# Dealing Fourier butterflies anew over projection units, and a third piece by VectorE in three units more

## The chip, the core and the metric

The kernel runs on one core of a Trainium2 chip. A core has TensorE (PE; its weight loads are listed as PEld), VectorE (DVE), ScalarE (ACT), GpSimd (POOL) and SyncE (SP, which only issues transfers here), each with a queue of its own that it works off in order, and 16 DMA engines. Engines wait for each other by semaphores. The metric is the device time of one execution in microseconds (us); lower is better.

## The reference

Two independent computations, side by side in the output. A is a memory-augmented attention over 2048 rows of 576 with 32 heads of 18, in 4 segments of 512; B is a filter in the two-dimensional Fourier space.

```python
def _A_ref(x, wq, wk, wv, wo, beta):
    q, k, v = ...            # x @ wq, x @ wk, x @ wv, split into heads and 4 segments
    phi = lambda t: jnp.where(t > 0, t + 1.0, jnp.exp(t))
    for s in range(N):
        qs, ks, vs = q[:, :, s], k[:, :, s], v[:, :, s]
        logits = jnp.einsum("bhqd,bhkd->bhqk", qs, ks) * scale + mask
        p = _softmax(logits, axis=-1)
        a_dot = jnp.einsum("bhqk,bhkd->bhqd", p, vs)
        num = jnp.einsum("bhld,bhde->bhle", phi(qs), M)
        den = jnp.einsum("bhld,bhd->bhl", phi(qs), z)[..., None] + 1e-6
        outs.append(g * num / den + (1.0 - g) * a_dot)
        M = M + jnp.einsum("bhld,bhle->bhde", phi(ks), vs)
        z = z + jnp.einsum("bhld->bhd", phi(ks))
    return o @ wo

def _B_ref(x, w_r, w_i):
    X = jnp.fft.rfft2(x, axes=(-2, -1)) * (w_r + 1j * w_i)
    return jnp.fft.irfft2(X, s=(S, D), axes=(-2, -1))
```

## The kernel before

The kernel has four stages, one after the other on TensorE: the forward transform of B, the projections of A (q, k and v), the inverse transform of B, and the attention of A. The order of instructions on each engine is written out by hand; what is issued first on an engine runs first there.

The 2048-point transform of B is cut into parts that are matmuls (forward and inverse stage) and parts of radix 4 that VectorE does on the array Z in on-chip memory: butterflies (L210), twiddle factors (L227 on VectorE, fed by L221 and L222 on ScalarE), the product with the filter (L247, L249, L253, L255). These parts are written as Python generators that yield after each VectorE instruction, 200 steps in all, which the class `Pace` deals out in small numbers between the work of A. Each step is one VectorE instruction on 128 x 580 numbers, but for one step in each set of twiddles that starts with ScalarE alone. 14 steps are dealt in the forward stage. `projections` (L540) deals all that are left but 8, and the inverse takes the rest.

`projections` runs four groups g of 512 rows. In each it runs 13 units i: nine of q and k (i = 0 to 8, `qk_unit`, L466), each 128 of the 1152 columns of q and k, then four of v (i = 9 to 12, `v_unit`, L503), each 128 rows. A matmul in full single precision is made of 14 passes over high and low parts (`passes`, L454).

A q or k unit's result lies in a bank of PSUM, the accumulation memory. There are five such banks for these units (tag `pj`); they are used in turn, and a v unit takes two of them, one for each half of its columns. The result is written as three bfloat16 pieces into `sp3`. ScalarE copies the first piece out (L476). VectorE subtracts it from the bank in place (L483). ScalarE copies the second piece (L487). The third piece is made in one of two ways: either TensorE subtracts the second piece in the bank, by a matmul with a negative unit matrix `nid` (L491), and ScalarE copies the rest out (L492); or VectorE subtracts and writes in one instruction (L489). Before the change VectorE does it in the odd units of groups 1 to 3. In most units ScalarE and VectorE also compute phi (L479, L480, L482), and the phi of k is transposed on TensorE (L500). On v units TensorE also adds up M and z (L523), VectorE masks them (L531) and GpSimd adds them on (L535 to L539).

The loop of `projections` in unit i issues: the first half of unit i on TensorE; one advance of every unit that is open; 70% of the steps of the unit's share w; one more advance; the second half of unit i; the other 30% of w. By the two advances, unit i-1 gets its L476 and phi in the first and L482 and L483 in the second, and unit i-2 gets L487 in the first and its third piece in the second. On VectorE the order in unit i is thus: the 70%, L489 of unit i-2 if it has one, L482 and L483 of unit i-1, the 30%. The share is in proportion to a weight, 1 for a unit of q or k and 2.1 for one of v (L560).

In the last group a hook issues the splitting of Z for the inverse (`ysplit`, L278): ScalarE copies the high part Y (L284), and VectorE subtracts for the low part (L285) in the units i = 10, 11 and 12. Before it splits, it takes steps until the butterflies that it needs are issued. The inverse starts with matmuls on Y (L300), of which ScalarE copies the high part (L330) and VectorE subtracts the low part (L332), and goes on with L311.

Of the kernel before, what the change touches and what calls it, by code (L numbers as in the profile page):

```python
# [389 lines left out]
class ATT:  # L390
# [63 lines left out]
    def passes(s,out,g,wt,cs,xs,swap):  # L454

        wh,wl=s.wh[wt],s.wl[wt]; xh=[s.xh[g,t] for t in range(5)]; xl=[s.xl[g,t] for t in range(4)]
        L=[]
        for t in range(4):
            L+=[(wh[:,t,cs],xh[t][:,xs]),(wh[:,t,cs],xl[t][:,xs]),(wl[:,t,cs],xh[t][:,xs])]
        L+=[(wh[:,4,cs],xh[4][:,xs]),(wl[:,4,cs],xh[4][:,xs])]  # L460
        if swap:
            L=[(b,a) for a,b in L]
        for i,(a,b) in enumerate(L):
            s.nc.tensor.matmul(out,a,b,start=i==0,stop=i==len(L)-1)  # L464
            if i==6 and not swap: yield
    def qk_unit(s,g,mt,tp,pp):  # L466

        nc=s.nc
        ps=pp.tile([128,512],F32,name="pj",tag="pj")
        yield from s.passes(ps,g,"wqk",slice(128*mt,128*mt+128),slice(0,512),False)  # L470
        yield
        sp3=tp.tile([128,3,512],BF,name="sp3",bufs=3)
        r0=0 if (g>0 or mt>4) else 64
        r1=128 if (g<3 or mt<4) else 64
        if (g==0 and mt<4) or (g==3 and mt>4): r1=r0
        nc.scalar.copy(sp3[:,0],ps)  # L476
        if r1>r0:
            e=tp.tile([128,512],F32,name="ex")
            nc.scalar.activation(e[r0:r1],ps[r0:r1],AF.Relu,scale=-1.0)  # L479
            nc.scalar.activation(e[r0:r1],e[r0:r1],AF.Exp,scale=-1.0)  # L480
        yield
        if r1>r0: nc.vector.scalar_tensor_tensor(e[r0:r1],ps[r0:r1],0.0,e[r0:r1],op0=OP.max,op1=OP.add)  # L482
        nc.vector.tensor_tensor(ps,ps,sp3[:,0],op=OP.subtract)  # L483
        qr=min(r1,128 if mt<4 else (64 if mt==4 else 0))
        if qr>r0: nc.sync.dma_start(s.pqD[g][128*mt:128*mt+qr],e[:qr])
        yield
        nc.scalar.copy(sp3[:,1],ps)  # L487
        yield
        if g>0 and mt%2: nc.vector.tensor_tensor(sp3[:,2],ps,sp3[:,1],op=OP.subtract)  # L489
        else:  # L490
            nc.tensor.matmul(ps,s.nid,sp3[:,1],start=False,stop=True,skip_group_check=True)  # L491
            nc.scalar.copy(sp3[:,2],ps)  # L492
        nc.sync.dma_start(s.qkD[g][128*mt:128*mt+128],sp3)
        if r1<=r0: return
        k0=max(r0,0 if mt>4 else (64 if mt==4 else 128))
        if k0>=r1: return
        n=r1-k0; c0=128*mt+k0-576
        pt=pp.tile([128,4,128],F32,name="ptr",tag="pt")
        for tb in range(4):
            nc.tensor.transpose(pt[:,tb,:n],e[k0:r1,128*tb:128*tb+128],s.ident[k0:r1,k0:r1])  # L500
        yield
        nc.scalar.copy(s.pk[:,:,c0:c0+n],pt[:,:,:n])
# [37 lines left out]
    def projections(s,xp,tp,pp,wv,pace,hook):  # L540

        live=[]
        s.nid=wv.tile([128,128],BF,name="nid"); s.nc.scalar.activation(s.nid,s.ident,AF.Copy,scale=-1.0)
        lw=s.load_w("wv",576,wv,xp,288,"xl",4)
        def advance():
            for l in list(live):
                try: next(l)
                except StopIteration: live.remove(l)
        tot=pace.left-8
        for g in range(4):  # L550
            if g<3: xq=[s.xprep(g+1,t,(xp,s.x0)[g%2],xp,[128,512],"xst",2) for t in range(5)]
            for i in range(13):
                u=s.qk_unit(g,i,tp,pp) if i<9 else s.v_unit(g,i-9,tp,pp)
                if i==4 and g<3: s.pk=tp.tile([128,4,576],F32,name="pk",bufs=1)
                next(u)
                hook(g,i)
                next(lw,None); next(lw,None)
                if g<3 and i in (4,6,8,10,12): next(xq[(i-4)//2])
                if g<3 and i in (1,3,5,7,9): next(xq[(i-1)//2])
                w=tot/(36+16*2.1)*(1.0 if i<9 else 2.1)  # L560
                advance()
                pace.take(w*.7)
                advance()
                next(u)
                pace.take(w*.3)
                live.append(u)
        while live: advance()
# [573 lines left out]
```

## Time and profile before

| | |
|---|---|
| runs shown | 718.73, 719.6, 716.9 us; median 718.73 |
| profiled execution | 715.83 us, its span 714.1 us |
| PE busy | 678.0 us, 95% of the span |
| DVE busy | 552.8 us, 77% |
| ACT busy | 444.4 us, 62% |
| POOL busy | 209.1 us, 29% |
| granted TensorE clock | 1.00 over the span |

The span is the time from the first to the last instruction that the profiler records. Matmuls overlap: one lasts longer than the time until the next starts, so a busy TensorE is read by how many matmuls start in a stretch, and a wait of TensorE by the time from one start to the next. Times in a row of a time line are counted from the start of the span.

### The profile page before, as it was taken

Reading aid. Unit: us, or ns where it says so; the run is one execution under the profiler, and the core shown is the slowest. Engines: PE = TensorE matmul, PEld = TensorE weight load, DVE = VectorE, ACT = ScalarE, POOL = GpSimd, SP = SyncE. Lnnn points to the kernel's source line nnn. Section 1 sums busy time; section 2 is a strip of 40 time slices with the busy share of each in tenths; the row PEclk is TensorE's granted clock in tenths of the full one; section 3 lists DMA queues with packets and bytes.
Section 4 is the critical chain, followed back from the end, with each engine's and each line's share of the span. In section 5 each row is a group of like instructions: output and inputs, shape, how many; then the busy total and the mean of one; then the engine's idle time right before and its main releaser. Section 6 shows DMA issues by size and latency. Waiting matters only on the chain.

```text
span 714.1 us, 14181 instructions
## 1 busy us (share of the span) xinstructions
PE 678.0 (95%) x4867; PEld 498.0 (70%) x4867; DVE 552.8 (77%) x1227; ACT 444.4 (62%) x1000; POOL 209.1 (29%) x409
## 2 busy tenths in 40 slices
PE   5999999999999999999999999999999999998997
PEld 4999769879879779999844444444566445664677
DVE  6999989799799699787587878887566876668153
ACT  3657685575575564444487777777556676568631
POOL 2110000100100211465165434554242762237200
PEclk9999999999999999999999999999999999999999
DMA  9876536545473568899547666676547765341331
GB/s 344 277 224 200 157 125 192 182 162 181 136 238 127 164 209 278 204 232 226 167 112 180 173 163 148 176 177 172 134 121 181 172 164 132 104 138 43 99 100 66
DMA packets 83245, 121.04 MB, mean 170 GB/s; under 512 B 11353, under 2 KB 50631, under 8 KB 83037
## 3 DMA queue, kind: packets, MB, share of 16 engines
q1 hardware_dynamic: 76580, 104.11, 51.4%
q0 software_dynamic: 6592, 16.03, 8.1%
q8 instruction: 38, 0.62, 0.4%
q14 instruction: 35, 0.28, 0.1%
HBM read 81.78 MB, written 38.24 MB: 168 GB/s over the span
## 4 chain that ended last, share of the span: by engine, by line
PE 66%; DVE 14%; ACT 6%; DMA 6%; issue 4%; POOL 2%; SPq 0%; DVEq 0%; ACTq 0%; POOLq 0%
PE pv L716 9%; PE pj L464 7%; PE po L858 7%; PE pjv L464 7%; PE s L643 5%; PE i L300 4%; PE i L311 4%; PE s L651 4%; PE s L686 3%; DVE junk L647 2%; PE s L690 2%; PE po L888 2%; DMA x<-qkD 2%; DVE pj L483 2%; PE c L163 2%
## 5 line engine op out<-in xcount | busy, mean ns | idle before, releaser
L647 DVE CUSTOM_DVE_ANT_0 junk<-s,mask 128x512 bf16<-128x512 f32 (+1 forms) x256 | 141.5, 553 | 58.1 <-PE s L643 46.6
L653 DVE TENSOR_REDUCE mx<-s 128x4 f32<-128x512 f32 x128 | 87.9, 686 | 16.3 <-PE s L652 14.8
L687 ACT ACTIVATE P<-s 128x512 f32<-128x512 f32 x128 | 77.2, 603 | 23.3 <-PE s L686 20.4
L716 PE MATMUL pv<-P,vs 128*32 128x512 f32 (+3 forms) x1024 | 82.0, 438 | 0.0
L692 ACT ACTIVATE P<-s 128x512 f32<-128x512 f32 x128 | 77.0, 602 | 6.7 <-PE s L691 3.6
L696 ACT ACTIVATE P<-s 128x256 f32<-128x256 f32 x128 | 49.6, 387 | 50.1 <-PE s L695 50.1
L699 POOL TENSOR_SCALAR_AFFINE_SELECT P<-P 128x512 f32<-128x512 f32 x116 | 69.3, 633 | 6.2 <-ACT P L687 6.0
L716 PEld LDWEIGHTS pv<-P,vs 128*32 128x32 f32 x1024 | 26.8, 109 | 44.7 <-issue 42.0
L464 PE MATMUL pj<-x,wqkh 128*128 128x512 f32 x162 | 55.9, 406 | 0.0
L513 POOL MEMSET vt<- 128x32 f32 x16 | 2.4, 161 | 150.9 <-PE pm L523 123.7
L210 DVE TENSOR_TENSOR t<-Z 128x580 f32<-128x580 f32 x64 | 46.1, 755 | 0.1
L210 DVE TENSOR_TENSOR Z<-t 128x580 f32<-128x580 f32 x64 | 45.8, 755 | 0.1
L643 PE MATMUL s<-Ks,Qs 108*128 108x512 bf16 (+1 forms) x128 | 42.2, 329 | 0.0
L487 ACT CAST sp<-pj 128x512 bf16<-128x512 f32 x36 | 21.0, 585 | 30.0 <-DVE pj L483 30.0
L142 PE MATMUL f<-ftab,eh 128*128 128x290 f32 (+1 forms) x160 | 31.2, 313 | 8.9 <-DMA ftab<-ftab 8.9
L300 PE MATMUL i<-civ,Y 128*128 128x256 f32 (+1 forms) x288 | 37.9, 284 | 1.3 <-DVE T L332 1.3
L300 PEld LDWEIGHTS i<-civ,Y 128*128 128x128 f32 (+1 forms) x288 | 35.8, 181 | 1.6 <-DVE T L332 1.6
L311 PE MATMUL i<-itab,T 128*128 128x290 f32 (+1 forms) x224 | 36.4, 311 | 0.0
L668 POOL CAST mh<-mg 128x16 bf16<-128x16 f32 x32 | 6.8, 214 | 100.0 <-ACT mg L666 69.3
L464 PEld LDWEIGHTS pj<-x,wqkh 128*128 128x128 f32 x162 | 30.4, 188 | 7.7 <-issue 1.0
L464 PE MATMUL pj<-x,wqkl 128*128 128x512 f32 x90 | 35.6, 395 | 0.0
L464 PE MATMUL pj<-xh,wqkh 128*128 128x512 f32 x90 | 35.6, 395 | 0.0
(214 smaller groups left out, 1854.5 us busy)
## 6 DMA issues: line engine op xcount, KB each, us to landing
qkD<-sp SPq DMA_DIRECT2D x36, 384.0 KB
Ks<-qkD SPq DMA_DIRECT2D x72, 144.0 KB
x<-qkD SPq DMA_DIRECT2D x60, 144.0 KB
Qs<-qkD SPq DMA_DIRECT2D x60, 144.0 KB
xin<-xb SPq DMA_DIRECT2D x16, 384.0 KB
cfw<-cfw POOLq DMA_DIRECT2D x16, 384.0 KB, 4.3
civ<-civ POOLq DMA_DIRECT2D x16, 384.0 KB, 7.6
vs<-vD SPq DMA_DIRECT2D x16, 330.0 KB
```

Source lines behind the costliest of these rows:

```text
L210: v.tensor_tensor(o,a,b,op=op)
L300: nc.tensor.matmul(p[:m,k],Y[i][:,q,c*128:c*128+m],cc[:,hl,o:o+256],start=n==0,stop=n==5)
L311: nc.tensor.matmul(p,x,t,start=n==0,stop=n==6)
L464: s.nc.tensor.matmul(out,a,b,start=i==0,stop=i==len(L)-1)
L643: nc.tensor.matmul(out,Q[:108,h,128*i:128*i+128],K[:108,h,:128*(i+1)],start=True,stop=True)
L647: nc.vector.tensor_tensor_reduce(out=junk[:,:w],in0=src,in1=s.mask[:,512-w:],scale=1.0,scalar=-3.0e38, op0=OP.add,op1=OP.max,accum_out=s.m ...
L653: nc.vector.tensor_reduce(out=s.mx[k][:,hh],in_=pa.rearrange("p (b c) -> p b c",c=128),axis=mybir.AxisListType.X,op=OP.max)
L687: nc.scalar.activation(P[0][:,hh],p0,AF.Exp,scale=SC)
L692: nc.scalar.activation(P[1][:,hh],p1,AF.Exp,scale=SC)
L699: if k<29: nc.gpsimd.affine_select(out=x,in_=x,pattern=pat+[[1,128]],compare_op=OP.is_ge,fill=0.0,base=0,channel_multiplier=-1)
L716: nc.tensor.matmul(s.pvt[32*hh:32*hh+32,128*j:],vt[:,j,19*h:19*h+32],mv[0][:,hh,mv[1]],start=j==0,stop=j==2,skip_group_check=True)
L858: nc.tensor.matmul(ps,a[t][:r,c],b[:r,t,w],start=i==0,stop=i==14)
```

## The change

A unit's third piece is made by VectorE in unit 8 of groups 1 to 3 too, beside the odd units. The share of steps is worked out with other weights: 2.6 for a unit of v instead of 2.1, and 0.75 instead of 1 for a unit of q or k whose third piece is VectorE's. The sum of the weights in the divisor follows (15 units have 0.75).

```diff
+    def third(s,g,mt): return g>0 and (mt%2 or mt==8)
     def qk_unit(s,g,mt,tp,pp):
...
         nc.scalar.copy(sp3[:,1],ps)
         yield
-        if g>0 and mt%2: nc.vector.tensor_tensor(sp3[:,2],ps,sp3[:,1],op=OP.subtract)
+        if s.third(g,mt): nc.vector.tensor_tensor(sp3[:,2],ps,sp3[:,1],op=OP.subtract)
         else:
             nc.tensor.matmul(ps,s.nid,sp3[:,1],start=False,stop=True,skip_group_check=True)
             nc.scalar.copy(sp3[:,2],ps)
...
-                w=tot/(36+16*2.1)*(1.0 if i<9 else 2.1)
+                w=tot/(36-15*.25+16*2.6)*(2.6 if i>8 else .75 if s.third(g,i) else 1.0)
                 advance()
                 pace.take(w*.7)
                 advance()
```

## The prediction

> **What bounds the kernel now.** I read the page's head first, then a table of stages, the waits of TensorE, the time line of VectorE at the end of the stage, and the groups for prices. The change touches one stage, the projections, which run from 70.8 us to about 284 us. In the table the columns after the stretch are its length and the busy time of PE, PEld, DVE, ACT and POOL with their instruction counts, then granted clock, DMA share and GB/s.
>
> ```profile
> span 714.1 us, 14181 instructions
> ```
> ```profile
> 70.80:106.20 35.40, 32.98 (x148) 25.14 (x147) 32.49 (x55) 28.10 (x63) 0.35 (x4) 1.00 0.43 135
> ...
> 124.50:159.10 34.60, 33.94 (x164) 26.87 (x163) 29.47 (x50) 22.35 (x42) 3.25 (x14) 1.00 0.50 168
> 159.10:177.80 18.70, 18.63 (x144) 18.37 (x143) 18.53 (x28) 9.86 (x23) 0.34 (x4) 1.00 0.60 193
> ...
> 230.50:264.00 33.50, 32.67 (x151) 25.96 (x150) 26.70 (x45) 18.86 (x37) 3.75 (x10) 1.00 0.56 178
> 264.00:284.00 20.00, 19.41 (x150) 19.08 (x148) 19.84 (x32) 9.86 (x23) 5.27 (x16) 1.00 0.88 287
> ```
>
> The stretches are: q and k units of group 0, q and k of group 1, v of group 1, q and k of group 3, v of group 3. TensorE is busy nearly throughout, so it sets the pace; it loses 2.42, 0.66, 0.07, 0.83 and 0.59 us in them. VectorE has slack in q and k of groups 1 and 3 (5.1 and 6.8 us), but none in the last v stretch (0.16 us idle in 20). That last row speaks against putting more there.
>
> Where TensorE loses time in q and k shows in its time line, with the idle time before an instruction and its releaser in brackets:
>
> ```profile
> 80.09 0.38 PE L491 MATMUL pj<-sp,nid 128*128 128x512 bf16 x1 [0.93 <-ACT sp L487]
> ...
> 95.00 0.38 PE L491 MATMUL pj<-sp,nid 128*128 128x512 bf16 x1 [0.78 <-ACT sp L487]
> ...
> 99.94 0.38 PE L491 MATMUL pj<-sp,nid 128*128 128x512 bf16 x1 [0.71 <-ACT sp L487]
> ...
> 149.23 0.38 PE L491 MATMUL pj<-sp,nid 128*128 128x512 bf16 x1 [0.66 <-ACT sp L487]
> ...
> 202.08 0.38 PE L491 MATMUL pj<-sp,nid 128*128 128x512 bf16 x1 [0.38 <-ACT sp L487]
> ...
> 247.76 0.38 PE L491 MATMUL pj<-sp,nid 128*128 128x512 bf16 x1 [0.20 <-ACT sp L487]
> ...
> 255.30 0.38 PE L491 MATMUL pj<-sp,nid 128*128 128x512 bf16 x1 [0.63 <-ACT sp L487]
> ```
>
> All seven are the matmul of L491, late because ScalarE's L487 waited for VectorE's L483, queued behind butterflies. A matmul lasts 0.39 us but the next starts 0.23 us after it, so each bracket hides 0.16 us more; the seven cost 4.29 + 7 x 0.16 = 5.4 us.
>
> VectorE in turn runs dry where a v stretch ends:
>
> ```profile
> 130.87 0.69 DVE L482 SCALAR_TENSOR_TENSOR ex<-pj,ex 128x512 f32<-128x512 f32 x1 [3.46 <-ACT ex L480]
> ...
> 184.00 0.69 DVE L482 SCALAR_TENSOR_TENSOR ex<-pj,ex 128x512 f32<-128x512 f32 x1 [2.25 <-ACT ex L480]
> ...
> 236.63 0.69 DVE L482 SCALAR_TENSOR_TENSOR ex<-pj,ex 128x512 f32<-128x512 f32 x1 [3.71 <-ACT ex L480]
> ```
>
> These 2 to 4 us at the start of groups 1, 2 and 3 are what the first three v stretches can take more of for nothing.
>
> **The change part by part.** Prices: groups, shapes kept apart, then three rows of the chain of waits.
>
> ```profile
> L210 DVE TENSOR_TENSOR Z<-t 128x580 f32<-128x580 f32 x56 | 39.8, 755 | 0.1
> L483 DVE TENSOR_TENSOR pj<-pj,sp 128x512 f32<-128x512 f32 x36 | 24.8, 688 | 0.1
> ...
> L492 ACT CAST sp<-pj 128x512 bf16<-128x512 f32 x24 | 13.9, 578 | 4.0 <-PE pj L491 3.6
> ...
> L489 DVE TENSOR_TENSOR sp<-pj,sp 128x512 bf16<-128x512 f32 x12 | 8.2, 681 | 0.0
> ```
> ```profile
> 80.46 3.27 PE pj L464 x14
> 83.73 0.23 PE pj L491
> ...
> 108.84 3.71 PE pjv L464 x28
> ```
>
> A q or k unit costs TensorE 3.27 us, a v unit 3.71, the L491 matmul 0.23. Four butterflies in a row end after 2.77 us (row below), so one costs VectorE (2.77 - 0.755) / 3 = 0.67; L489 and L483 start 0.60 apart, so 0.60 each.
>
> *The new deal.* By the code there are 200 steps, 14 are dealt before the stage, 8 kept for after it: 178 to deal. Before, a unit of q or k gets 178/69.6 = 2.56 and one of v 5.37. After, 178/73.85 = 2.41, 1.81 where VectorE makes the third piece, and 6.27 in v. I counted which step falls where. Between the first and the fifth unit's L483 of groups 1, 2 and 3 there are now 8, 8 and 9 steps instead of 11, 10 and 11. The single late L491 of group 1 (0.66 + 0.16 = 0.82), that of group 2 (0.54) and the second of group 3 (0.79) need less than 0.67 x 2 of relief, so I take them as gone: 2.15 us gained. The first of group 3 has as many steps ahead as before (5) and stays. In group 0 the count of steps up to unit 8's L483 is the same (26), and the first late L491 has the same steps before it. The second loses two ScalarE operations of a twiddle that move a unit on; I take its 0.78 as gained and leave the others, between 0 and 2.9 us (all three brackets with their 0.16).
>
> *More in v, groups 0 to 2.* Four steps more per stretch, 2.7 us, hidden in the 2.25 to 3.71 us of VectorE's idle above. Were that cover gone, each step would cost 0.67. What is late next is the L482 of the following group's first unit and, behind it, that unit's L483, L487 and L491.
>
> *Third piece in unit 8 of groups 1 to 3.* It removes 0.23 us of TensorE and 0.58 of ScalarE, adds 0.60 of VectorE. In group 1 the matmul also opened a hole: 165.16 to 165.74 for a 0.13 us matmul, so 0.45 gained there, 0.23 in group 2. But unit 8's bank of the five is now freed by VectorE's L489, which stands behind the first butterflies of the v stretch, and the fifth allocation after it, the first half of the third v unit, takes that bank. For group 1:
>
> ```profile
> 159.30 0.29 PE L464 MATMUL pjv<-wvh,xh 128*128 128x288 f32 x1
> ...
> 165.16 0.29 PE L464 MATMUL pjv<-wvl,xh 128*128 128x288 f32 x1
> ...
> 165.74 0.60 PE L500 MATMUL ptr<-ident,ex 128*128 128x128 f32 x4
> ...
> 168.04 0.29 PE L464 MATMUL pjv<-wvh,xh 128*128 128x288 f32 x1
> ```
> ```profile
> 164.16 0.69 DVE L483 TENSOR_TENSOR pj<-pj,sp 128x512 f32<-128x512 f32 x1
> ```
>
> Unit 8 ends at 159.30, the third v unit starts at 168.04, or 8.3 us later without the matmul and its hole. VectorE ended L483 of unit 8 at 164.76. With four steps fewer since the group began (2.7 us) and the group starting 0.8 earlier, that is 161.3. Behind it stand 7 steps (4.7), L437 (0.6) and L489 (0.6): the bank is free at 167.2. TensorE, 0.8 + 0.8 earlier, wants it at 157.7 + 8.3 = 166.0. A new wait of 1.2 us: the whole TensorE queue stands behind it, and VectorE is not held. Bounds: 0, up to 3.1 (rivals). In group 2 only 5 steps stand between; I take nothing.
>
> So up to the end of group 3's unit 8, TensorE is ahead by 0.78 + 0.82 + 0.45 - 1.2 + 0.54 + 0.23 + 0.79 = 2.4 us.
>
> *The last v stretch.* No idle time to fill here: VectorE also splits Y.
>
> ```profile
> 261.88 0.69 DVE L483 TENSOR_TENSOR pj<-pj,sp 128x512 f32<-128x512 f32 x1
> 262.48 2.10 DVE L210 TENSOR_TENSOR t<-Z 128x580 f32<-128x580 f32 x3
> ...
> 265.85 0.68 DVE L489 TENSOR_TENSOR sp<-pj,sp 128x512 bf16<-128x512 f32 x1
> 266.45 0.69 DVE L483 TENSOR_TENSOR pj<-pj,sp 128x512 f32<-128x512 f32 x1
> ...
> 278.46 1.09 DVE L285 TENSOR_TENSOR Y<-Z,Y 128x512 fp32r<-128x512 f32 x2
> 279.47 2.77 DVE L210 TENSOR_TENSOR Z<-t 128x580 f32<-128x580 f32 x4
> ...
> 282.83 0.68 DVE L332 TENSOR_TENSOR T<-i,T 128x512 fp32r<-128x512 f32 x1
> ...
> 284.00 0.69 DVE L332 TENSOR_TENSOR T<-i,T 128x512 fp32r<-128x512 f32 x1
> ```
> ```profile
> 263.92 0.30 PE L464 MATMUL pjv<-wvh,xh 128*128 128x288 f32 x1
> ...
> 278.99 4.42 PE L300 MATMUL i<-civ,Y 128*128 128x256 f32 x36
> 284.75 2.41 PE L300 MATMUL i<-civ,Y 128*128 128x256 f32 x18 [1.34 <-DVE T L332]
> ```
>
> From 262.48 VectorE works without a pause to the second L332, and TensorE resumes at 284.75 when that is done: VectorE sets the end of the stage. From unit 7's L483 to the first L332 stood 24 steps; now 29 do, and a second L489: 5 x 0.67 + 0.60 = 4.0 us more. The L483 of unit 7 can itself be about 0.4 us earlier against TensorE, since the butterflies before it are fewer. So TensorE resumes 4.0 - 0.4 - 2.4 = 1.2 us later than before. The bank wait comes here too. On the clock of before, VectorE is through unit 7's L483 at 262.1, through 5 steps, L489 and unit 8's L483 at 266.7, and through 6 steps, a Y split (1.01, from 278.46 to 279.47), 4 steps and L489 at 275.0; TensorE wants the bank at 263.92 + 2 x 3.71 = 271.3 and pauses 3.7 us. Its v units then end at 282.4 and the inverse's first 30 matmuls, by 36 in 4.42, at 286.1, with ScalarE's copy 286.7; VectorE's second L332 comes at 287.6 all the same. So the pause costs nothing here.
>
> *After it.* Two steps fewer stay for the inverse, where VectorE has spare time; nothing. Sum: +1.2 us. The profiled execution took 715.83 us (714.1 and 1.7 around), so it would become 717.0; the median shown is 718.73, 2.9 above it, and I carry +1.2 over: 719.9.
>
> **Rivals.**
> 1. *Faster.* All seven late L491 go (5.4), with 0.45 and 0.23, and no bank wait: 6.1 ahead, less 3.6 at the end, -2.5 us, 716.2. For it: VectorE's load in q and k falls in all groups. Against: group 0 has the same steps before its first stall.
> 2. *Slower by the bank.* VectorE reaches unit 8's L483 as late after the unit's last matmul as now (164.76 - 159.30 = 5.5 us). L489 then ends 5.5 + 5.9 = 11.4 after it in group 1 and, with two steps fewer, 10.0 in group 2, against the 8.3 from which it decides: waits of 3.1 and 1.7, 3.6 more than counted, +4.8 us, 723.5. For it: VectorE's total work in the stage rises by 1.8 us. Against: fewer steps ahead of it.
> 3. *A cold array.* TensorE's pause of 3.7 us in the last v stretch would be longer than any wait it has here after the start (1.34). If matmuls ran at half rate for as long again, TensorE would lose 1.9 us, of which 0.9 is covered by VectorE being later still: +1.0 on the forecast, 720.9. Against: the granted clock is 1.00 in every stretch above. The Trainium skill, TensorE: Matmul & The Clock Gate, in the part on the HAM clock gate, says that an idle window of about 3.4 us brings the array to half its clock until it has been busy as long; no run here shows such a pause yet.
>
> **How the numbers follow.** Forecast 0.52, faster rival 0.17, bank 0.20, cold array 0.05, the rest 0.06 spread. The three runs spread by about 1.4 us to either side, and half a per cent, 3.6 us (715.1 and 722.3), is what a measurement of this kernel can tell. Below 715.1 fall a quarter of the first rival and some of the rest: 0.08. Above 722.3 fall three quarters of the bank case, a little of the forecast and the rest: 0.21. Within: 0.71. The range reaches to the faster and the bank rival and half of that spread beyond them: 715.4 to 724.2; the forecast's own is 718 to 722.
>
> **What would show it.** Right: the bracketed waits of L491 in groups 1 to 3 gone but for group 3's first; a wait of a v matmul for L489 near 166 us, and one of 3 to 4 us near 270; VectorE idle longer in q and k of group 3; VectorE without a pause from unit 7's L483 to L332, and TensorE resuming near 286 us. Wrong: if TensorE resumes before 284, the last stretch was not VectorE's; if no v matmul waits for L489, the bank rule fell; if L491 still waits as now, the deal moved the wrong steps.

## The result and the profile after

| | before | after |
|---|---|---|
| runs | 718.73, 719.6, 716.9, 719.24 | 725.66, 727.87, 724.32, 725.5 |
| median | 718.99 us | 725.58 us |
| span of the profiled execution | 714.1 us | 723.9 us |

The changed kernel is slower: ratio 1.0105, 95% interval 1.0076 to 1.0134, 6.6 us by the medians. 719.9 was forecast, with 715.4 to 724.2 as the range.

The page's head shows at once something that the kernel before does not have, a slice in which the granted clock (PEclk) is not full:

```profile
span 723.9 us, 14176 instructions
...
PEclk9999999999999999799999999999999999999999
```

The waits of TensorE, with what it waited for, the total, how often, and the longest:

```profile
PE i L300 <- DVE T L332: 7.6, 1, 7.6
...
PE pj L492 <- ACT sp L488: 1.5, 5, 0.6
...
PE pjv L464 <- ACT vt L517: 1.2, 1, 1.2
...
PE pj L492 <- DVE t L210: 0.9, 1, 0.9
...
PE pj L492 <- DVE Z L227: 0.7, 1, 0.7
```

(Lines after L463 carry one number more than before: the third-piece matmul is L492 here.) The waits of the late third-piece matmuls fell from 4.3 us to 3.1, but the single wait for L332 at the end of the stage grew from 1.34 to 7.6 us. TensorE's time line there:

```profile
280.39 4.43 PE L300 MATMUL i<-civ,Y 128*128 128x256 f32 x36
292.46 4.21 PE L300 MATMUL i<-civ,Y 128*128 128x256 f32 x18 [7.64 <-DVE T L332]
296.47 2.65 PE L311 MATMUL i<-itab,T 128*128 128x290 f32 x14
```

The same 18 matmuls took 2.41 us before and take 4.21 behind the wait. The table of stretches says why (the third number from the right is the clock):

```profile
284.00:286.00 2.00, 0.82 (x8) 0.59 (x6) 1.97 (x3) 1.04 (x3) 1.83 (x1) 1.00 0.72 165
286.00:288.00 2.00, 0.00 (x0) 0.00 (x0) 2.00 (x4) 0.00 (x0) 1.63 (x3) 0.89 0.76 179
288.00:290.00 2.00, 0.00 (x0) 0.00 (x0) 2.00 (x4) 0.00 (x0) 0.00 (x0) 0.50 1.00 260
```
```profile
292.40:295.00 2.60, 2.54 (x12) 2.54 (x13) 0.44 (x2) 0.00 (x0) 0.00 (x0) 0.50 0.00 0
295.00:297.00 2.00, 2.00 (x11) 2.00 (x11) 0.69 (x1) 1.54 (x4) 0.00 (x0) 0.50 0.00 0
297.00:300.00 3.00, 3.00 (x22) 3.00 (x22) 1.11 (x3) 0.99 (x4) 2.27 (x3) 0.87 0.00 0
```

TensorE stops at 280.39 + 4.43 = 284.8. A mean of 0.89 over 286 to 288 is full clock for 78% of it, so it falls to half at about 287.6, 2.7 us after the stop; by the mean of 0.87 it returns at about 297.8, 5.3 us after work resumed.

The two profiled executions already differ by 1.6 us where the projections begin (first matmul at 70.83 and 72.43 us), ahead of anything that was changed. Counted from there, TensorE resumes at 213.92 before and 220.03 after, 6.1 us later. VectorE on the way there:

```profile
261.50 0.70 DVE L484 TENSOR_TENSOR pj<-pj,sp 128x512 f32<-128x512 f32 x1 [1.52 <-ACT sp L477]
262.18 0.76 DVE L227 SCALAR_TENSOR_TENSOR Z<-Z,tw 128x580 f32<-128x580 f32 x1
265.66 0.76 DVE L227 SCALAR_TENSOR_TENSOR Z<-Z,tw 128x580 f32<-128x580 f32 x1 [2.72 <-ACT tw L222]
...
277.29 0.68 DVE L490 TENSOR_TENSOR sp<-pj,sp 128x512 bf16<-128x512 f32 x1
...
283.60 0.76 DVE L210 TENSOR_TENSOR Z<-t 128x580 f32<-128x580 f32 x1
284.28 1.94 DVE L285 TENSOR_TENSOR Y<-Z,Y 128x512 fp32r<-128x512 f32 x2
286.14 2.47 DVE L210 TENSOR_TENSOR Z<-t 128x580 f32<-128x580 f32 x3
288.54 2.09 DVE L210 TENSOR_TENSOR t<-Z 128x580 f32<-128x580 f32 x3
290.56 0.68 DVE L332 TENSOR_TENSOR T<-i,T 128x512 fp32r<-128x512 f32 x1
```

From unit 7's L484 to the first L332 it took 20.95 us before (261.88 to 282.83) and takes 29.06 now, 8.1 more. The five more steps and the L490 of unit 8 are the 4.0 of the forecast. The 2.72 us in brackets are new: VectorE waits for a twiddle's ScalarE part. And the pair of L285 and the three butterflies after it take 1.94 and 2.47 us where they took 1.09 and 2.10, 1.2 more. That is all but 0.2. Two rows of other engines give the causes, first ScalarE, then GpSimd:

```profile
264.37 0.59 ACT L477 CAST sp<-pj 128x512 bf16<-128x512 f32 x1 [0.60 <-ACT sp L488]
264.85 0.45 ACT L221 ACTIVATE tw<-Z 128x290 f32<-128x290 f32 x1
```
```profile
284.16 2.48 POOL L285 TENSOR_TENSOR Y<-Z,Y 128x512 fp32r<-128x512 f32 x2 [2.11 <-ACT Y L284]
```

The last twiddle stands in ScalarE's queue behind L477 of unit 8, which needs unit 8's last matmul. (The bracket of L477 names L488, which had ended at 263.77; it was TensorE's row below, which ends at 264.28, that came last.)

```profile
263.89 0.39 PE L464 MATMUL pj<-xh,wqkl 128*128 128x512 f32 x1
```

GpSimd's own split of Y, on the same kind of tile, runs just while VectorE's instructions are slow. In the kernel before, the same twiddles were done earlier, two of them already with short waits for the same L222, and GpSimd's split began only when VectorE was about to reach L332:

```profile
257.01 0.77 DVE L227 SCALAR_TENSOR_TENSOR Z<-Z,tw 128x580 f32<-128x580 f32 x1 [0.44 <-ACT tw L222]
258.66 0.76 DVE L227 SCALAR_TENSOR_TENSOR Z<-Z,tw 128x580 f32<-128x580 f32 x1 [0.88 <-ACT tw L222]
260.54 0.75 DVE L227 SCALAR_TENSOR_TENSOR Z<-Z,tw 128x580 f32<-128x580 f32 x1
```
```profile
282.70 1.93 POOL L285 TENSOR_TENSOR Y<-Z,Y 128x512 fp32r<-128x512 f32 x2 [2.14 <-ACT Y L284]
```

### The profile page after: what moved, and what is told of

It reads as the page before. It is cut to its first block, busy times and chain, and to the rows that moved or that the text cites. A ratio compares the mean times of both kernels' runs of the same rounds, so it can differ in the third digit from the quotient of the medians.

```text
span 723.9 us, 14176 instructions
## 1 busy us (share of the span) xinstructions
PE 680.4 (94%) x4864; PEld 501.4 (69%) x4864; DVE 556.6 (77%) x1230; ACT 443.5 (61%) x997; POOL 209.8 (29%) x409
## 4 chain that ended last, share of the span: by engine, by line
PE 72%; DVE 11%; DMA 7%; ACT 4%; issue 3%; POOL 2%; SPq 1%; DVEq 0%; ACTq 0%; POOLq 0%
PE pj L464 13%; PE pv L717 9%; PE pjv L464 6%; PE po L859 6%; PE s L644 5%; PE s L652 3%; PE f L142 3%; PE i L300 3%; PE s L687 3%; DMA yb<-yout 3%; DVE junk L648 3%; PE i L311 3%; PE c L163 3%; PE s L691 2%; PE po L889 2%
## 5 line engine op out<-in xcount | busy, mean ns | idle before, releaser
L300 PE MATMUL i<-civ,Y 128*128 128x256 f32 (+1 forms) x288 | 39.7, 292 | 7.6 <-DVE T L332 7.6
L300 PEld LDWEIGHTS i<-civ,Y 128*128 128x128 f32 (+1 forms) x288 | 37.4, 189 | 7.9 <-DVE T L332 7.9
L488 ACT CAST sp<-pj 128x512 bf16<-128x512 f32 x36 | 21.1, 585 | 28.5 <-DVE pj L484 28.4
L311 PE MATMUL i<-itab,T 128*128 128x290 f32 (+1 forms) x224 | 37.0, 315 | 0.2 <-DVE yout L319 0.2
L464 PE MATMUL pj<-xh,wqkl 128*128 128x512 f32 x90 | 35.5, 395 | 0.0
```

Source lines behind the costliest of these rows:

```text
L300: nc.tensor.matmul(p[:m,k],Y[i][:,q,c*128:c*128+m],cc[:,hl,o:o+256],start=n==0,stop=n==5)
L311: nc.tensor.matmul(p,x,t,start=n==0,stop=n==6)
```

## The experiments

Every ratio is against the kernel before, run on the same chip. The column "first L332" is counted from the first matmul of the projections in the profiled execution, "wait" is TensorE's wait for it.

| kernel | first L332, us | wait, us | median, us | ratio (95%) |
|---|---|---|---|---|
| before | 212.00 | 1.3 | | 1 |
| changed | 218.13 | 7.6 | 725.58 | 1.0105 (1.0076 to 1.0134) |
| deal_only | 218.05 | 4.0 | 724.67 | 1.0096 (1.0071 to 1.0121) |
| third_only | 212.91 | 3.2 | 721.07 | 1.0042 (1.0020 to 1.0064) |
| new_012 | 209.87 | 0.8 | 716.43 | 0.9990 (0.9966 to 1.0014) |
| new_3 | 219.32 | 8.3 | 725.62 | 1.0119 (1.0096 to 1.0142) |
| after_warm | 218.18 | 1.0, the rest filled | 723.21 | 1.0082 (1.0059 to 1.0105) |
| after_nopool | 216.93 | 6.4 | 726.18 | 1.0122 (1.0101 to 1.0144) |
| after_light3 | 210.85 | 0.8 | 718.36 | 1.0025 (0.9999 to 1.0050) |
| new012_light3 | 209.33 | 0.8 | 715.90 | 0.9974 (0.9950 to 0.9997) |
| third_warm | 212.91 | 0.8, the rest filled | 718.05 | 1.0012 (0.9988 to 1.0035) |
| after_tw | 215.35 | 6.3 | 722.07 | 1.0067 (1.0048 to 1.0086) |
| after_tw_nopool | 213.99 | 4.9 | 722.48 | 1.0061 (1.0031 to 1.0091) |

The kernel before had medians of 717.54, 717.80 and 717.19 us in the three sets of experiments.

**Which part, and where.** Four kernels split the change by its two edits and by groups.

deal_only, the changed kernel with

```diff
-    def third(s,g,mt): return g>0 and (mt%2 or mt==8)
+    def third(s,g,mt): return g>0 and mt%2
...
-                w=...(2.6 if i>8 else .75 if s.third(g,i) else 1.0)
+                w=...(2.6 if i>8 else .75 if s.third(g,i) or (g>0 and i==8) else 1.0)
```

> The new deal of steps to every unit, unit 8's third piece back on TensorE and ScalarE. Theory (VectorE sets the end of the projections, and the steps moved into the last v stretch are late there): nearly as slow as the changed kernel, +5 to +7 us on the kernel before, TensorE waiting 6 to 8 us for L332 and the granted clock falling below 1 behind that wait. Rival (the third piece in unit 8 is to blame): within 1.5 us of the kernel before, the wait for L332 at most 2.5 us.

third_only, the changed kernel with

```diff
-                w=tot/(36-15*.25+16*2.6)*(2.6 if i>8 else .75 if s.third(g,i) else 1.0)
+                w=tot/(36+16*2.1)*(1.0 if i<9 else 2.1)
```

> Unit 8's third piece by VectorE in groups 1 to 3, the deal of before. Theory: within 1 us of the kernel before, since it adds 0.6 us of VectorE to the last v stretch and takes 0.45 and 0.23 us from TensorE; the wait for L332 at 1.3 to 2.2 us. Rival (the third piece is to blame): +4 us or more.

new_012, the changed kernel with

```diff
-    def third(s,g,mt): return g>0 and (mt%2 or mt==8)
+    def third(s,g,mt): return g>0 and (mt%2 or (mt==8 and g<3))
...
+                if g==3: w=tot/(36+16*2.1)*(1.0 if i<9 else 2.1)
```

> The change in groups 0 to 2 alone; group 3 has the weights and the third pieces of before. Theory: the waits of L491 in groups 1 and 2 and unit 8's matmul are saved (0.8 + 0.45 + 0.54 + 0.23 = 2.0 us), the last stretch is as before: 1 to 2.5 us faster than the kernel before, the wait for L332 about 1 to 2 us. Rival (heavier v stretches cost in every group): +3 us or more, with waits of TensorE in groups 1 and 2.

new_3, the same the other way round (`mt==8 and g==3`, and the old share `if g<3`):

> The change in group 3 alone. Theory: the whole loss and none of the gain, +6 to +9 us on the kernel before, slower than the changed kernel by 0.5 to 2 us; wait for L332 of 6 to 10 us, granted clock at half behind it. Rival: under +3 us.

The deal alone is nearly as slow as the whole change, and group 3 alone is. In groups 0 to 2 the change does not cost: in new_012 L332 comes 2.1 us earlier than before and TensorE resumes 1.7 us earlier, but the time is only 0.1% lower, which is within the interval, where 1 to 2.5 us had been expected. The trace shows where the lead goes. From the stage's first matmul to the last of the program it takes 639.64 us, before 639.29: TensorE waits in the attention where the kernel before has no such waits, in the second row for a load of K.

```profile
399.31 0.38 PE L653 MATMUL s<-x,Qs 108*128 108x384 bf16 x2 [1.46 <-issue]
...
470.67 0.38 PE L653 MATMUL s<-x,Qs 108*128 108x384 bf16 x2 [0.75 <-DMA Ks<-qkD]
```

What the first waits for, and why the loads come late, stays open. In new_3 and deal_only TensorE's rows are:

```profile
292.15 4.21 PE L300 MATMUL i<-civ,Y 128*128 128x256 f32 x18 [8.31 <-DVE T L332]
```
```profile
272.25 0.38 PE L492 MATMUL pj<-sp,nid 128*128 128x512 bf16 x1 [2.73 <-ACT sp L488]
283.27 4.43 PE L300 MATMUL i<-civ,Y 128*128 128x256 f32 x36
291.69 4.21 PE L300 MATMUL i<-civ,Y 128*128 128x256 f32 x18 [4.00 <-DVE T L332]
```

deal_only splits the loss into two waits, 2.7 us at unit 8's own matmul and 4.0 at L332, but arrives at the same L332. The 4.0 was below the 6 to 8 expected, for that reason. The first of the two waits brings the clock down too, 0.9 us after work had resumed:

```profile
270.00:272.00 2.00, 0.00 (x0) 0.00 (x0) 2.00 (x4) 1.27 (x3) 0.00 (x0) 1.00 0.89 270
272.00:274.00 2.00, 1.75 (x10) 1.73 (x10) 1.97 (x5) 1.97 (x6) 0.00 (x0) 0.78 1.08 377
274.00:276.00 2.00, 2.00 (x11) 2.00 (x10) 2.00 (x4) 1.00 (x4) 0.00 (x0) 0.50 1.11 401
276.00:278.00 2.00, 2.00 (x15) 2.00 (x15) 2.00 (x4) 0.77 (x2) 0.00 (x0) 0.86 1.01 396
```

By the means of 0.78 and 0.86 it was at half from 273.1 to 276.6. third_only missed its expectation: 0.4% slower, not the same. Its rows show what I had not counted, TensorE first, then VectorE, GpSimd and the clock:

```profile
285.62 4.21 PE L300 MATMUL i<-civ,Y 128*128 128x256 f32 x18 [3.17 <-DVE T L332]
```
```profile
282.04 1.75 DVE L210 TENSOR_TENSOR t<-Z 128x580 f32<-128x580 f32 x1
```
```profile
281.99 2.24 POOL L285 TENSOR_TENSOR Y<-Z,Y 128x512 fp32r<-128x512 f32 x2 [2.12 <-ACT Y L284]
```
```profile
284.00:286.00 2.00, 0.38 (x1) 0.38 (x2) 1.91 (x4) 0.00 (x0) 1.28 (x3) 0.60 0.63 156
...
290.00:292.00 2.00, 2.00 (x13) 2.00 (x12) 0.43 (x1) 1.16 (x5) 1.75 (x3) 0.69 0.00 0
```

A butterfly of 1.75 us instead of 0.76 and a wait of 3.2 us, and again 4.21 us for the 18 matmuls: this wait, too, halved the clock, by the means of 0.60 and 0.69 from 284.4 to 291.2. The fall comes 2.0 us after TensorE stopped at 282.5.

**The clock.** Two kernels keep TensorE at work through the wait, with matmuls into a bank that nobody reads, issued ahead of the inverse's third block. after_warm is the changed kernel with

```diff
+            if u==2:
+                d=pp.tile([128,512],F32,name="dummy",tag="mt")
+                for _ in range(56): nc.tensor.matmul(d[:,:256],s.itab[:,0,0,0,:128],s.itab[:,0,0,0,:256],start=True,stop=True)
```

> The changed kernel with 56 matmuls into a bank that nobody reads, issued on TensorE ahead of the third column block's matmuls of the inverse, so that it works (about 6.6 us) where it waited 7.6 us for L332. Theory (a good part of the loss is the clock that the wait brings down): granted clock 1.00 there, 18 matmuls of L300 behind the wait in 2.4 us instead of 4.2, 14 of L311 in 2.0 instead of 2.6, the whole 2 to 3.5 us faster than the changed kernel, still 3 to 5 us slower than the kernel before. Rival (only the lateness of VectorE counts): no faster than the changed kernel.

third_warm is third_only with 20 of them:

> Unit 8's third piece by VectorE with the deal of before (the kernel that came out 0.4% slower, with a wait of 3.2 us for L332 and 18 matmuls of L300 behind it in 4.2 us), and 20 matmuls into a bank that nobody reads within that wait. Theory (the 0.4% is the clock that falls in a wait of 3.2 us, not the work of the third piece): granted clock 1.00, the 18 matmuls in 2.4 us, the whole within 1 us of the kernel before. Rival (VectorE's work itself): still 2 to 4 us slower.

In after_warm and in third_warm the 18 matmuls are fast again (the third row is third_warm's unread matmuls):

```profile
292.17 2.40 PE L300 MATMUL i<-civ,Y 128*128 128x256 f32 x18 [0.96 <-DVE T L335]
```
```profile
285.87 2.41 PE L300 MATMUL i<-civ,Y 128*128 128x256 f32 x18 [0.76 <-DVE T L335]
```
```profile
282.56 2.55 PE L328 MATMUL dummy<-itab 128*128 128x256 f32 x20
```

Counted from the stage's first matmul to the last of the program, after_warm's trace is 6.05 us behind the kernel before and the changed kernel's 8.20: 2.2 us less, with L332 where it was. By the ratios after_warm is 0.23%, 1.7 us, closer to the kernel before than the changed kernel, but the two intervals overlap, so the times alone do not show it. By the medians of its set it stayed 5.4 us behind the kernel before (723.21 against 717.80), and 3 to 5 had been expected. third_warm has third_only's L332 to the hundredth and is level with the kernel before; in the traces, counted in the same way, it is 0.7 us behind it and third_only 2.8. So in the traces most of third_only's loss is the clock. In the times the intervals of these two overlap as well, and the times of third_only's ten executions do not follow their mean clocks (718.83 us at 0.999, 722.17 at 0.998, 718.62 at 0.994); other differences between executions are as large.

**The steps.** after_light3 is the changed kernel with half the steps in the last v units, new012_light3 is new_012 with 0.8 of them:

```diff
+                if g==3 and i>8: w*=.5
                 advance()
                 pace.take(w*.7)
```

> The changed kernel with half the steps in the four last v units, so that about 9 steps go to the inverse instead. Theory (steps in the last v stretch are the loss): L332 about 6 us earlier against TensorE's start of the stage, the wait for it 1 to 2.5 us, granted clock 1.00, the whole within 1.5 us of the kernel before. Rival (the earlier groups lose): still +4 us or more.

> The change in groups 0 to 2, before's weights in group 3 and there 0.8 of them in the last four v units (about 4 steps go to the inverse). Theory: no wait for L332 any more (0.8 us gained on the kernel with the change in groups 0 to 2), 1.5 to 3 us faster than the kernel before. Rival (the inverse has no room for the steps): slower than the kernel with the change in groups 0 to 2, with waits of TensorE for L332 inside the inverse.

after_light3's first wait for L332, and the other two in the inverse:

```profile
283.74 2.41 PE L300 MATMUL i<-civ,Y 128*128 128x256 f32 x18 [0.76 <-DVE T L332]
...
307.66 1.68 PE L300 MATMUL i<-civ,Y 128*128 128x256 f32 x12 [0.79 <-DVE T L332]
...
327.80 1.69 PE L300 MATMUL i<-civ,Y 128*128 128x256 f32 x12 [0.89 <-DVE T L332]
```

Nine steps fewer took L332 from 218.13 to 210.85 and nearly all of the loss with it; the 7.3 us are 9 x 0.67 = 6.0 for the steps, and the 1.2 us of slow VectorE rows, which do not occur there. The steps are not free in the inverse, where they bring two more waits, 0.79 and 0.89 us, but cheap. new012_light3 is the one that beats both kernels, by 0.26% against before, with an interval that just excludes 1; its trace does not show the gain (0.8 us behind that of before, from the stage's first matmul to the last, with waits of 1.07 and 1.48 us for loads in the attention). Its wait for L332 stayed at 0.76, where none was expected, since ScalarE's L330 is now the last to come.

**The two unforeseen delays of VectorE.** after_tw issues the ScalarE parts of the last set of twiddles together:

```diff
-    def tws(s,L,inv):
+    def tws(s,L,inv,early=False):
...
-                if i==0: yield
-            if i>0:
+                if i==0 and not early: yield
+            if early and i<len(L)-1: continue
+            if early and i==len(L)-1: yield
+            while A if early else i>0 and len(A)>(i<len(L)):
...
-            yield from s.tws([(x[b],b*c) for b in (2,1,3)],True)
+            yield from s.tws([(x[b],b*c) for b in (2,1,3)],True,c==3)
```

> The changed kernel with the ScalarE parts of the last set of twiddles (L221, L222) issued together with the first, ahead of unit 8's L477. Theory (2.7 us of the lateness is VectorE waiting for a twiddle queued behind L477, which waits for unit 8): that wait is gone, the wait for L332 falls from 7.6 to about 5 us, the clock still falls, the whole 1.5 to 3 us faster than the changed kernel, that is 3.5 to 5.5 us slower than the kernel before. Rival (another wait takes its place): no change.

after_nopool takes GpSimd's split of Y away:

```diff
-                if u==0: s.ysplit(3)
+                if u==1: s.ysplit(3,nc.vector)
```

> The changed kernel with the fourth split of Y issued one step later and on VectorE instead of GpSimd. Theory (GpSimd's L285 slows VectorE's instructions on on-chip memory while both run): the instructions of VectorE ahead of L332 keep their 0.67 us apart, L332 comes about 1.2 us earlier, the whole 1 to 2 us faster than the changed kernel. Rival (no contention): no change within 0.5 us.

after_tw_nopool does both:

> Both at once: the early ScalarE twiddles, and the fourth split of Y later and on VectorE. Theory: the wait for L332 falls to about 3.7 us, near the length at which the clock falls; 2.5 to 5 us faster than the changed kernel, 2 to 4.5 us slower than the kernel before. Rival (the whole does not follow L332): within 1 us of the changed kernel.

after_tw, and then VectorE and TensorE of after_nopool:

```profile
288.34 3.93 PE L302 MATMUL i<-civ,Y 128*128 128x256 f32 x18 [6.29 <-DVE T L334]
```
```profile
284.80 1.08 DVE L285 TENSOR_TENSOR Y<-Z,Y 128x512 fp32r<-128x512 f32 x2
```
```profile
291.75 4.21 PE L300 MATMUL i<-civ,Y 128*128 128x256 f32 x18 [6.41 <-DVE T L332]
```

The early twiddles bring L332 2.78 us forward, as the 2.72 us wait said, and the time from 1.0105 to 1.0067. The wait fell only to 6.3 us, not to 5, since the pause of 1.2 us at the third v unit went too and TensorE reached the end sooner; with both edits it is 4.9 us where 3.7 had been expected, for the same reason. Without GpSimd's split the two L285 take 1.08 us again, not 1.94, and L332 comes 1.20 us earlier; with both edits it comes 4.14 earlier. So it is shown that VectorE's rows are slow because of GpSimd's split, but the 1 to 2 us expected do not show in the time (1.0122 against 1.0105, 1.0061 against 1.0067). In the profiled executions the end comes 1.2 and 0.9 us earlier, counted from the stage's first matmul; that is less than 0.2% of the time, which these intervals can neither show nor rule out.

## Why the prediction was wrong, point by point

*VectorE sets the end of the stage, and the last v stretch has no room:* right. The 4.0 us for five steps and an L489 are in the trace, and halving the steps there removed the loss.

*"VectorE works without a pause":* this step failed, and with it the term of 4.0 us for the last stretch, which measured 8.1. It was read from the time line of before, where nothing stood between unit 7's L483 and L332. The lines just ahead of that, 257.01 and 258.66, already had VectorE waiting for ScalarE's twiddles. But a new deal does not only add steps; it moves the kinds of step. The last two of a set of three twiddles slid from units 7 and 8 to unit 9, behind a ScalarE copy that waits for unit 8: 2.7 us, shown by after_tw. Later VectorE work also came to run beside GpSimd's split of Y: 1.2 us.

*The 2.4 us that TensorE would be ahead:* 1.4 at the first v unit of group 3 (263.92 - 70.83 before, 264.12 - 72.43 after). The forecast had taken off 1.2 for a bank wait that did not come (next point), so 3.6 of gain gave 1.4. Group 0, from which 0.78 was expected, put TensorE 0.5 behind: its first two stalls shrank from 0.93 and 0.78 to 0.57 and 0.20, the third stayed, and a new one of 0.87 came at 105.66. Group 1 gave the 0.8 for its L491 and the 0.45 for unit 8; group 2 gave 0.4 and nothing for unit 8, not 0.54 and 0.23. In group 3 the second stall shrank from 0.63 to 0.40 only.

*The bank wait:* wrong. No v matmul waits for VectorE's third piece. The third v unit takes the bank that was released first, by the first v unit's copy to `vt`: unit 8's L490 ends at 278, and the third v unit had started at 272.87, after a wait for that copy. The counted 1.2 us in group 1 and the 3.7 us pause in group 3 did not exist; the wait for the copy took 1.2 us in group 3. That the error of 1.2 us hid part of the too large gain elsewhere is luck.

*The cold array:* listed with a chance of 0.05, priced at 1.0 us, and looked for in the wrong wait. It is the magnifier: it comes behind the wait for L332 itself and costs 1.8 us on 18 matmuls of L300 and 0.6 on 14 of L311 (2.06 before), 2.4 together, and 2.2 by the trace of after_warm. The Trainium skill's rule (TensorE: Matmul & The Clock Gate, Part 1: The HAM clock gate), an idle window of about 3.4 us, agrees with the runs only roughly: a wait of 4.0 us brought the clock to half, but so did waits of 3.2 and 2.7, and in third_only it fell 2.0 us after the last matmul. The measurements decide. The longest wait behind the forward stage that left the clock at 1.00 is 1.5 us (new_012); none lies between 1.5 and 2.7. With 1.3 us before the change, the kernel stood at most 1.4 us from a wait that halves the clock.

In sum, TensorE's resumption was forecast 1.2 us later and came 6.1 later: 2.7 for the twiddles, 1.2 for VectorE's slow rows beside GpSimd, and 0.8 for the smaller gain ahead (unit 7's L484 came 2.0 us earlier, not 2.4 + 0.4); 0.2 is left over. The cold array adds 2.4. That makes 8.5 us, against 8.2 by which the two profiled executions differ from the stage's first matmul to the last; the medians show 6.6, and the runs of before spread by 2.7 us. (The lower end of the range, 716.2 less 0.7, should have been 715.5; it decides nothing.)

## What to carry to other kernels

When steps are dealt anew, count not only how many fall where, but what each of them waits for on the other engines' queues; a stretch without a pause in the old trace may get one. The last stretch before a stage that needs the result is different from the earlier ones, and should get its own, smaller share: the same weights did no harm in groups 0 to 2 and lost 1.2% in group 3. Where TensorE waits 1 to 2 us for another engine, ask what happens if the wait doubles: its price may then not be the wait alone, since the clock can fall behind it.

## What the runs showed of the hardware

Waits of TensorE of 2.7 us (deal_only) and 3.2 us (third_only) already halved the granted clock. It fell 2.0 us after the last matmul in third_only and 2.7 in the changed kernel, and in deal_only's first wait 0.9 us after work had resumed. Full speed came back 5.3 us after work had resumed in the changed kernel and 4.3 after deal_only's first wait. By the rows above the half clock lasted 10.2 us in the changed kernel (287.6 to 297.8), 6.8 in third_only (284.4 to 291.2) and 3.4 in deal_only (273.1 to 276.6): three, two and one times 3.4. That looks as if the clock were set once in 3.4 us; it is a reading of these traces that no run here was made to test. If it is right, whether a wait of 2 to 3 us costs anything depends on where it falls. Twenty matmuls of 0.12 us that nobody reads were enough to prevent it in third_warm.

VectorE instructions with two operands in on-chip memory stretch while GpSimd runs such an instruction: a butterfly from 0.76 to 1.75 us (third_only), two L285 from 1.09 to 1.94 (the changed kernel). The Trainium skill, SBUF — State Buffer, in the section SBUF: two separate sides, describes the pair of ports that the two engines share as a lock that is held for a whole instruction; the added 1.0 us fits a wait for the first of GpSimd's two subtractions there (2.24 us for both).
